# Gated mix of sliding-window attention and a gated feed-forward, forward and backward: Wo's gradient built in the last stage, and a new order of the first loads

## The chip, the cores and the metric

The kernel runs on one core of a Trainium2 chip. Times are device microseconds of one execution; the time of a kernel is the median over its runs. A profile is one further execution, recorded by the hardware; its span runs from the first to the last instruction of the program.

Engines: TensorE (PE in the profile; its weight loads are PEld), VectorE (DVE), ScalarE (ACT), GpSimd (POOL) and SyncE (SP), which here only issues transfers. Each engine works through its own instructions in order. A transfer is issued from the queue of one of them and is moved by 16 DMA engines.

## What is computed

With x of 2048 rows and 512 columns, 32 heads of 16, and a window of 256:

```python
g = sigmoid((x * gate_w).sum(-1))            # one gate a row
a = attention(x, wqkv, wo)                   # softmax(q k^T / 4 | window) v, then @ wo
b = ((relu(x@Wg)) * (x@Wu)) @ Wd             # F = 1376
out = g * a + (1 - g) * b
```

Returned are `out` and, for a given `grad_out` (go), the gradients of x, wqkv, wo, Wg, Wu, Wd and gate_w. With da = g * go and o the attention's output before `wo`, the gradient of wo is `o^T @ da`, a product of 512x2048 by 2048x512. It is this product that the change moves. Inputs and outputs are bf16.

## The kernel before

Rows are cut into NT = 16 tiles of 128; four tiles make a group (NTG = 4 groups of 512 rows). D = 512 is cut into DC = 4 chunks of 128 columns, which are also 4 chunks of 8 heads each; F into FC = 11 chunks, the last of which overlaps the one before.

**Start and stage 1** (to about 240 us of the profile): a program written out by hand, in which each engine's order is the order of the code. SP loads the first group of x in two halves (line 241); ScalarE's queue loads the first 256 columns of Wg and Wu (lines 242 and 243) and the gate's weights; SP goes on with x of group 1, a transpose of Wd's first chunk by DMA (`turn_wd`), and then by turns go and x of the groups (lines 255 to 262), and the rest of Wg and Wu. Per group `turn_x` transposes x on TensorE through a PSUM tile (two tiles of rows share one), VectorE copies the first half and ScalarE the second to `x_T`. `gate_col` gives the gate, `db_rows` multiplies go by 1 - g (lines 295 and 297, two of four tiles on each engine), `turn_db` transposes that. The main loop runs over 44 pairs of F's chunk and group; per pair it makes gate, up and dh products, multiplies them, transposes them by DMA, stores them to `hgu_d`, and adds up the weights' gradients. `make_da` makes da of a tile, and `turn_da` stores it to `da_d` in DRAM (line 320) and transposes it into `da_T` by DMA.

**Attention** (about 242 to 690 us): the four chunks of heads, one after another, each with 46 turns. A turn makes scores S and gradients of the probabilities D for four heads and two blocks, exp on ScalarE (line 747), masks on GpSimd (line 757), a product on VectorE (line 764), sums over rows on TensorE (lines 781, 783), transposes of the probabilities (TensorE at line 818, DMA at line 810), and pieces of dk and dv (lines 495, 498). The rows of dq, dk, dv and o of a chunk stand side by side in `rows_st` (`sts[c]`), which `spill` stores to `dqkvo_d`. One turn is written out behind the other; the position fixes the order on all queues.

Between these, background work is put in: `project_parts` of the next group, and the gradients of the chunk before, from `grad_parts`: four pieces for wqkv (384 columns, line 603) and, ahead of them, the part number DC for wo (512 columns, line 606). Each piece has a price in us; a credit per turn, from the prices left and the turns left, says how many pieces a turn gets. For wo's part, `grad_parts` loads all of da from `da_d` at turn 12 or so of each chunk: six loads of 256 KB on SP, two more from GpSimd's queue later (line 576). `late` holds weights for the last stage, one issued on every second turn.

**The seam** (about 690 to 711 us): no turns are left; the last chunk's gradients run (`early_group`, and `grad_parts` with `rest`). Its da comes by two loads of 512 KB (lines 871, 872) and four of 256 KB. The first group's data for the last stage are loaded by SP in the same stretch, W_up's last transposes behind them. `clear("Wu")` is a memset on GpSimd of the padded rows of what these transposes write.

**The last stage** (to the end): 16 tiles, in pairs that share loads (`load_group`, one pair ahead). Per tile TensorE makes bps = h Wd (11 matmuls, line 1117), aps = o wo (4, line 1121), and dx in `dxps` from 34 matmuls (lines 1147, 1173). From aps and bps come `out` and, by way of GpSimd's product with go (line 1133), the gate's derivative dz. VectorE adds dz's term to dxps (`dx_sb`, line 1179) and the rows of dx are stored. bps and aps have one PSUM buffer each, dxps has two. Here a scheduler may move instructions between engines' queues a little.

Of the kernel before, what the change touches and what calls it, by code (L numbers as in the profile page):

```python
# [22 lines left out]
def kernel(  # L23
# [20 lines left out]
    nc = tc.nc  # L44
# [54 lines left out]
    da_d = dram.tile([S, D], BF, name="da_d")  # L99
# [105 lines left out]
    with ExitStack() as p1, tc.manual_schedule():  # L205
# [36 lines left out]
        nc.scalar.dma_start(Wg_sb[:, :, 0:W0], Wg_v[:, :, 0:W0])  # L242
        nc.scalar.dma_start(Wu_sb[:, :, 0:W0], Wu_v[:, :, 0:W0])
# [27 lines left out]
        def turn_x(tg):  # L271
            for half in range(2):
                t0 = tg * TPG + 2 * half
                pt = ps1.tile([P, DC, 2, P], BF, tag="tr", bufs=2, name="ptx")
                for tt in range(2):
                    for c in range(DC):
                        nc.tensor.transpose(pt[:, c, tt, :], x_r[:, t0 + tt, c * P:(c + 1) * P], ident[:])
                evac(x_T[tg][:, :, 2 * half * P:(2 * half + 2) * P], pt[:].rearrange("p c t q -> p c (t q)"), ("dve", "act")[half])
# [40 lines left out]
        def turn_da(t):  # L319
            nc.sync.dma_start(da_d[t * P:(t + 1) * P, :], da_in[t][:])  # L320
# [150 lines left out]
    if True:  # L471
# [95 lines left out]
        def grad_parts(c, rest=None):  # L567
            out = []
            rows = {}

            def load_da(i, eng):
                pool, tag, bufs = (wk, "das", 2) if i in (4, 5) else (gwp, "dar", 4)
                a = pool.tile([P, 2, D], BF, tag=tag, bufs=bufs, name="dar")
                for e in range(2):
                    rows[2 * i + e] = a[:, e, :]
                eng.dma_start(a[:], da_d[i * 2 * P:(i + 1) * 2 * P, :].rearrange("(t p) d -> p t d", p=P))

            for i in range(6 if rest is None else 4):
                load_da(i, nc.sync)
            if rest is not None:  # L580
                rows.update(rest)
            hold = {}
            step = 2 if rest is None else 4

            def store(part, ws):
                if part < DC:
                    to = out_2[part * P:(part + 1) * P, :].rearrange("p (a n) -> p a n", a=3)[:, :, c * P:(c + 1) * P]
                else:
                    to = out_3[c * P:(c + 1) * P, :]
                return lambda: (nc.sync if rest is None else nc.gpsimd).dma_start(to, ws[:])  # L590

            def piece(part, t0, first, last):
                if first and rest is not None and part < DC:
                    if "SD"[part // 2] not in hold:
                        hold["SD"[part // 2]] = ps.tile([P, 2, 4, P], F32, tag="SD"[part // 2], bufs=1, name="wps")
                    hold[part] = hold["SD"[part // 2]][:, part % 2, 0:3, :]
                elif first:
                    hold[part] = ps.tile([P, 3, P] if part < DC else [P, D], F32, tag="tr", bufs=2, name="wps")[:]
                wps = hold[part]
                for t in range(t0, t0 + step):  # L600
                    go_, no_ = first and t == t0, last and t == t0 + step - 1
                    if part < DC:
                        nc.tensor.matmul(wps, lhsT=x_r[:, t, part * P:(part + 1) * P], rhs=sts[c][:, t, 0:3, :],  # L603
                                         start=go_, stop=no_)
                    else:
                        nc.tensor.matmul(wps, lhsT=sts[c][:, t, 3, :], rhs=rows[t], start=go_, stop=no_)  # L606
                if part == DC and rest is None and t0 + 12 < NT:
                    ev.setdefault(turn + 1, []).append(("load", lambda: load_da(t0 // 2 + 6, nc.gpsimd)))
                if not last:
                    return None  # L610
                if part < DC:
                    ws = (gwp if rest is None else S2["t6"]).tile([P, 3, P], BF, tag="ws", bufs=2 if rest is None else 5, name="ws")
                    share(ws[:], wps, 3 * P)
                    return store(part, ws)
                ws = (gwp if rest is None else S2["t6"]).tile([P, D], BF, tag="ws", bufs=2 if rest is None else 5, name="ws")
                share(ws[:], wps, D)
                return store(part, ws)

            if rest is None:
                parts = [(DC, 0, NT)] + [(p, 0, NT) for p in range(DC)]  # L620
            else:
                for a, b in ((0, NT - 4), (NT - 4, NT)):
                    if a:
                        out += [(DC, t0, t0 == 0, t0 + 4 == NT) for t0 in range(0, NT, 4)]
                    out += [(p, t0, t0 == 0, t0 + 4 == NT) for p in (0, 2, 1, 3) for t0 in range(a, b, 4)]
                return [lambda a=a: piece(*a) for a in out]
            for part, a, b in parts:
                out.append([(0.324 if part < DC else 0.432,
# [583 lines left out]
```

## Time and profile before

| | us |
|---|---|
| median of 3 runs | 894.38 |
| the runs | 887.89, 894.38, 899.25 |
| the profiled execution | 886.93 |
| its span | 885.2 |

Mean granted TensorE clock over the span: 0.998. Lines of the profile are read so: a group or a row names line, engine and operation, what it writes `<-` what it reads, and the shape; "x8" is how many instructions stand in a merged row; in a timeline the two numbers ahead are the start and the duration, and the bracket behind gives the idle time of the engine before it and what ended it. In the busy times by stretch, the numbers behind the stretch are its length and busy time (instructions) by engine, and at the end the granted clock, the mean share of time that the DMA engines were busy and GB/s. A row of transfers names destination and source, queue, count, size of one and the median time from issue to landing. Matmuls are pipelined: a 128x512 matmul has a duration of 379 ns in the records, while they start about 215 ns apart.

### The profile page before, as it was taken

Reading aid. Unit: us, or ns where it says so; the run is one execution under the profiler, and the core shown is the slowest. Engines: PE = TensorE matmul, PEld = TensorE weight load, DVE = VectorE, ACT = ScalarE, POOL = GpSimd, SP = SyncE. Lnnn points to the kernel's source line nnn. Section 1 sums busy time; section 2 is a strip of 40 time slices with the busy share of each in tenths; the row PEclk is TensorE's granted clock in tenths of the full one; section 3 lists DMA queues with packets and bytes.
Section 4 is the critical chain, followed back from the end, with each engine's and each line's share of the span. In section 5 each row is a group of like instructions: output and inputs, shape, how many; then the busy total and the mean of one; then the engine's idle time right before and its main releaser. Section 6 shows DMA issues by size and latency. Waiting matters only on the chain. (4 is left out here: it accounts for less than half of the span.)

```text
span 885.2 us, 29234 instructions
## 1 busy us (share of the span) xinstructions
PE 847.1 (96%) x12415; PEld 557.1 (63%) x12545; DVE 504.3 (57%) x758; ACT 386.2 (44%) x558; POOL 485.0 (55%) x894
## 2 busy tenths in 40 slices
PE   7999999999989999999999999999899999999998
PEld 4556655665557877777777767777677744444443
DVE  4445433333367888877778887787777323232222
ACT  5522222223266676766557655567455311111111
POOL 1645444444357787877668776687676532222221
PEclk9999999999999999999999999999999999999999
DMA  9999999998857999999978999899999999777750
GB/s 278 235 188 218 217 220 223 233 215 194 188 91 119 158 148 160 167 153 172 204 122 146 150 194 189 137 179 159 192 193 182 256 265 269 190 192 191 192 118 25
DMA packets 442156, 161.95 MB, mean 183 GB/s; under 512 B 361640, under 2 KB 439176, under 8 KB 442024
## 3 DMA queue, kind: packets, MB, share of 16 engines
q1 hardware_dynamic: 437896, 152.20, 90.9%
q0 software_dynamic: 2544, 7.34, 2.9%
q8 instruction: 98, 1.61, 0.7%
q10 hardware_dynamic: 1584, 0.53, 0.3%
q14 instruction: 34, 0.28, 0.1%
HBM read 38.44 MB, written 38.34 MB: 87 GB/s over the span
## 5 line engine op out<-in xcount | busy, mean ns | idle before, releaser
L764 DVE TENSOR_TENSOR PP<-PP,D 128x1024 bf16<-128x1024 bf16 (+1 forms) x184 | 219.2, 1191 | 68.2 <-POOL PP L757 24.7
L747 ACT ACTIVATE PP<-S 128x1024 bf16<-128x1024 f32 (+1 forms) x184 | 185.2, 1007 | 100.1 <-PE D L714 49.3
L757 POOL TENSOR_SCALAR_AFFINE_SELECT PP<-PP 128x512 bf16<-128x512 bf16 (+1 forms) x188 | 143.8, 766 | 90.1 <-ACT PP L747 87.4
L74 DVE COPY p<-pt 128x1024 bf16<-128x1024 bf16 x167 | 114.4, 685 | 13.0 <-PE pt L818 12.9
L357 POOL TENSOR_TENSOR hgu<-rg,upm 128x512 bf16<-128x512 bf16 x44 | 50.8, 1155 | 120.5 <-DVE upm L355 103.5
L818 PE MATMUL pt<-ident,PP 128*128 128x128 bf16 x1512 | 114.6, 219 | 0.9 <-issue 0.9
L781 PE MATMUL BA<-KV,PP 128*128 128x33 bf16 x1440 | 106.9, 180 | 3.7 <-ACT BAs L72 2.8
L781 PEld LDWEIGHTS <-PP 128*128 128x128 bf16 x1440 | 85.8, 96 | 31.1 <-issue 12.3
L783 PE MATMUL BA<-KV,PP 128*128 128x17 bf16 x1440 | 102.6, 170 | 0.7 <-issue 0.7
L397 PE MATMUL wps<-hgu_r,x_r 128*128 128x256 bf16 x640 | 96.0, 273 | 0.7
L495 PE MATMUL CD<-rq,p 128*128 128x32 bf16 x1440 | 94.9, 176 | 0.0
L498 PE MATMUL CD<-rq,p 128*128 128x16 bf16 x1440 | 93.6, 169 | 0.0
L783 PEld LDWEIGHTS <-PP 128*128 128x128 bf16 x1440 | 84.8, 96 | 10.7 <-issue 6.4
L818 PEld LDWEIGHTS <-PP 128*128 128x128 bf16 x1512 | 86.3, 97 | 1.2 <-issue 1.2
L714 PE MATMUL S<-zT,K 32*128 32x128 bf16 (+3 forms) x1056 | 77.9, 239 | 5.3 <-ACT PP L747 1.3
L495 PEld LDWEIGHTS <-p 128*128 128x128 bf16 x1440 | 80.7, 95 | 0.3
L498 PEld LDWEIGHTS <-p 128*128 128x128 bf16 x1440 | 80.5, 96 | 0.3
L397 PEld LDWEIGHTS <-x_r 128*128 128x128 bf16 x640 | 62.6, 98 | 28.6
L714 PE MATMUL D<-zT,V 32*128 32x128 bf16 (+3 forms) x1056 | 72.4, 238 | 5.8 <-DVE PP L764 5.2
L355 DVE SCALAR_TENSOR_TENSOR upm<-rg,ups 128x512 bf16<-128x512 bf16 x44 | 30.3, 689 | 79.8 <-PE ups L342 54.8
L1124 ACT COPY a_sb<-aps 128x512 f32<-128x512 f32 x16 | 9.4, 586 | 145.0 <-issue 133.1
L365 POOL TENSOR_TENSOR hgu<-dh_sb,rg 128x512 bf16<-128x512 bf16 x44 | 58.7, 1334 | 9.0 <-ACT dh_sb L363 9.0
(145 smaller groups left out, 1480.6 us busy)
## 6 DMA issues: line engine op xcount, KB each, us to landing
hgu_d<-hgu SPq DMA_DIRECT2D x44, 384.0 KB, 3.3
dqkvo_d<-rows_st SPq DMA_DIRECT2D x14, 512.0 KB, 4.7
dar<-da_d SPq DMA_DIRECT2D x22, 256.0 KB, 5.1
duT_g<-hgu_d SPq DMA_DIRECT2D x8, 640.0 KB, 6.0
dgT_g<-hgu_d SPq DMA_DIRECT2D x7, 640.0 KB
gt<-hgu_d SPq DMA_DIRECT2D x7, 640.0 KB, 5.9
p<-PP SPq DMA_TRANSPOSE x171, 4.2
out_dram<-wst SPq DMA_DIRECT2D x20, 128.0 KB, 3.0
```

The costliest lines, as they stand in the source:

```text
L74: nc.vector.tensor_copy(out, in_)
L365: nc.gpsimd.tensor_tensor(out=k.hgu[:, 2, :], in0=dh_sb[:], in1=k.rg[:], op=ALU.mult)
L397: nc.tensor.matmul(acc["w"][:, c, :], lhsT=x_r[:, t, c * P:(c + 1) * P], rhs=k.dgu_r[:, :, i, :], start=(go_ and c % 2 == 0), stop=no_, sk ...
L495: nc.tensor.matmul(cd[0][:, h, :], lhsT=p2[:, 0, pr, :], rhs=rq[:, h, 0:2 * Dh], start=cd[1], stop=True, skip_group_check=True)
L498: nc.tensor.matmul(cd[0][:, h, 0:Dh], lhsT=p2[:, 1, pr, :], rhs=rq[:, h, 2 * Dh:3 * Dh], start=False, stop=True, skip_group_check=True)
L714: nc.tensor.matmul(dst, lhsT=proj[(u.c, kb // TPG)][nm + ("", "1")[par]][rows[par], (kb % TPG) * P:(kb % TPG + 1) * P], rhs=proj[(u.c, qb ...
L747: nc.scalar.activation(two[:].rearrange("p x a b q -> p x a (b q)")[:, :, 0, 0:n], flat(us[0].S[:], n), ACT.Exp)
L757: nc.gpsimd.affine_select(out=out, in_=out, compare_op=ALU.is_ge, fill=0.0, base=0 if up else -1, pattern=[[0, 2], [0, b1 - b0], [1 if up ...
L764: nc.vector.tensor_tensor(out=v(1), in0=v(0), in1=flat(vs[0].D[:], n), op=ALU.mult)
L781: nc.tensor.matmul(BA[:, h, 0:33], lhsT=u.PP[:, 0, 2 * i + pr, :], rhs=kv[:, kb % TPG, h, 1:34], start=(first and pr == 0), stop=True, ski ...
L783: nc.tensor.matmul(BA[:, h, 33:50], lhsT=u.PP[:, 1, 2 * i + pr, :], rhs=kv[:, kb % TPG, h, 0:17], start=False, stop=True, skip_group_check ...
L818: nc.tensor.transpose(pt[:, a, b if u.nb == 2 else 2 * u.x + b, :], u.PP[:, a, b, :], ident[:])
```

## The change

Wo's gradient leaves `grad_parts` and is added up in the last stage, over all 16 tiles, in four PSUM tiles. da is made there anew by ScalarE from go (`da_b`), and o's rows come from `dqkvo_d` by a new load per tile (`o_g`). `da_d`, its 16 stores and all its loads go. To make room in PSUM, dxps has one buffer for two, and a small transpose at the end uses aps's. Of the new product, a tile's four matmuls are issued a tile later, behind aps of the next tile; the last tile's at once. At the last tile the four sums are copied (two on ScalarE, two on VectorE) and stored.

In the background work of attention, the part for wo is gone, the list of jobs per group of four tiles becomes (0, 2, 1, 1) for (0, 1, 2, 2), P2 has 14 buffers for 12, and in the last chunk `late` is issued on every fourth turn up to row tile 12.

At the start, all of x is issued ahead of Wd's transpose and of go; the first columns of Wg and Wu come behind the first group of x on SP and no more on ScalarE's queue; and the second half of the first group's copy to `x_T` is split between VectorE (two of four columns' chunks) and ScalarE.

```diff
-        nc.scalar.dma_start(Wg_sb[:, :, 0:W0], Wg_v[:, :, 0:W0])
-        nc.scalar.dma_start(Wu_sb[:, :, 0:W0], Wu_v[:, :, 0:W0])
+        nc.sync.dma_start(Wg_sb[:, :, 0:W0], Wg_v[:, :, 0:W0])
+        nc.sync.dma_start(Wu_sb[:, :, 0:W0], Wu_v[:, :, 0:W0])
...
-        load_x(1)
+        for tg in range(1, NTG):
+            load_x(tg)
         turn_wd(0)
-        load_go(0)
-        load_x(2)
-        load_go(1)
-        load_x(3)
-        load_go(2)
-        load_go(3)
+        for tg in range(NTG):
+            load_go(tg)
...
-                evac(x_T[tg][:, :, 2 * half * P:(2 * half + 2) * P], pt[:].rearrange("p c t q -> p c (t q)"), ("dve", "act")[half])
+                for c0, c1, eng in ((0, DC, "dve"),) if half == 0 else ((0, DC, "act"),) if tg else ((0, 2, "dve"), (2, DC, "act")):
+                    evac(x_T[tg][:, c0:c1, 2 * half * P:(2 * half + 2) * P],
+                         pt[:, c0:c1, :, :].rearrange("p c t q -> p c (t q)"), eng)
...
-            nc.sync.dma_start(da_d[t * P:(t + 1) * P, :], da_in[t][:])
...
-                p2 = pools["p2"].tile([P, 2, 4, P], BF, tag="P2", bufs=12, name="p2")[:]
+                p2 = pools["p2"].tile([P, 2, 4, P], BF, tag="P2", bufs=14, name="p2")[:]
...
+            o_g = S2["g6"].tile([P, GT, DC, P], BF, tag="o_g", name="o_g")
+            for t in range(GT):
+                t0 = (g * GT + t) * P
+                nc.sync.dma_start(o_g[:, t, :, :], dqkvo_d[t0:t0 + P, :].rearrange("p (c a n) -> p c a n", c=DC, a=4)[:, :, 3, :])
             nc.sync.dma_start(go_g[:] if g == 0 else go_g, go_d[gsl, :].rearrange("(t p) d -> p t d", p=P))
...
-                        for _ in range(((2, 1, 0, 0) if c == 0 else (0, 1, 2, 2))[j // TPG]):
+                        for _ in range(((2, 1, 0, 0) if c == 0 else (0, 2, 1, 1))[j // TPG]):
...
-                if late and (late[0] is not load_wo or turn > NI) and (not us or turn % 2 == 1):
+                if late and (late[0] is not load_wo or turn > NI) and (not us or turn % (4 if us[0].c == DC - 1 and us[0].q < 12 else 2) == 1):
...
+            wo_ps = [ps6.tile([P, D], F32, name=f"wo_ps{c}") for c in range(DC)]
+            pending_wo = []
+
+            def add_dwo(t_, o_, da_):
+                for c in range(DC):
+                    nc.tensor.matmul(wo_ps[c][:], lhsT=o_[:, c, :], rhs=da_[:], start=(t_ == 0), stop=(t_ == NT - 1))
...
+                    da_b = t6.tile([P, D], BF, tag="da_b")
+                    nc.scalar.mul(da_b[:], go_g[:, tl, :], g_all[:, t:t + 1])
+                    pending_wo.append((t, o_g[:, tl, :, :], da_b))
+                    while pending_wo and (pending_wo[0][0] < t or t == NT - 1):
+                        add_dwo(*pending_wo.pop(0))
                     a_sb = t6.tile([P, D], F32, tag="a_sb")
...
-                    dxps = ps6.tile([P, D], F32, tag="dxps", bufs=2)
+                    if t == NT - 1:
+                        for c in range(DC):
+                            ws = t6.tile([P, D], BF, tag="wo_s", bufs=DC, name="wo_s")
+                            evac(ws[:], wo_ps[c][:], ("act", "dve")[c % 2])
+                            nc.sync.dma_start(out_3[c * P:(c + 1) * P, :], ws[:])
+                    dxps = ps6.tile([P, D], F32, tag="dxps", bufs=1)
...
-                            dgw_t = ps6.tile([P, P], BF, name="dgw_t")
+                            dgw_t = psa.tile([P, P], BF, tag="aps", bufs=1, name="dgw_t")
```

In `grad_parts`, the loads of da (`load_da`, `rows`), the part number DC and its stores are taken out, and what is left keeps its order: four parts of 16 tiles for chunks 0 to 2, and in the seam the first twelve tiles of each part ahead of the last four.

More of the change, by code (lines that the diff above doesn't have):

```diff
@@ L599, in piece @@
                 wps = hold[part]
                 for t in range(t0, t0 + step):
[L601 to L606, printed above, removed]
@@ L607, in piece @@
-                if part == DC and rest is None and t0 + 12 < NT:
-                    ev.setdefault(turn + 1, []).append(("load", lambda: load_da(t0 // 2 + 6, nc.gpsimd)))
+                    nc.tensor.matmul(wps, lhsT=x_r[:, t, part * P:(part + 1) * P], rhs=sts[c][:, t, 0:3, :],
+                                     start=first and t == t0, stop=last and t == t0 + step - 1)
                 if not last:
                     return None
[L611 to L626, printed above, removed]
@@ L627, in grad_parts @@
[L627 to L631 removed]
+                ws = (S2["t6"] if seam else gwp).tile([P, 3, P], BF, tag="ws", bufs=4 if seam else 2, name="ws")
+                share(ws[:], wps, 3 * P)
+                to = out_2[part * P:(part + 1) * P, :].rearrange("p (a n) -> p a n", a=3)[:, :, c * P:(c + 1) * P]
@@ L936, in background @@
             def background():
[L937 removed]
+                price, f, more = bg.pop(0)
                 put = f()
```

75 lines of the change are left out of this document (24 added, 51 removed).

## The prediction

> **What bounds the kernel now.** I read the page's busy times first, then the busy times by stretch, then the chain of waits, and only then single engines.
>
> ```profile
> span 885.2 us, 29234 instructions
> ...
> PE 847.1 (96%) x12415; PEld 557.1 (63%) x12545; DVE 504.3 (57%) x758; ACT 386.2 (44%) x558; POOL 485.0 (55%) x894
> ```
> ```profile
> 0.00:20.00 20.00, 15.12 (x141) 9.29 (x144) 8.25 (x15) 10.45 (x16) 3.45 (x11) 1.00 0.99 266
> ...
> 100.00:140.00 40.00, 39.74 (x241) 23.90 (x245) 16.20 (x25) 11.62 (x20) 18.01 (x15) 1.00 0.96 223
> ...
> 348.10:462.50 114.40, 108.47 (x2496) 81.87 (x2518) 90.77 (x129) 70.86 (x98) 84.71 (x188) 1.00 1.03 163
> ...
> 735.00:885.00 150.00, 145.83 (x719) 67.17 (x732) 43.77 (x97) 16.88 (x30) 31.52 (x41) 1.00 0.67 164
> ```
>
> The columns after a stretch are its length and the busy time of TensorE, its weight loads, VectorE, ScalarE and GpSimd, then clock, DMA share, GB/s. TensorE fills stage 1 (39.74 of 40), attention for one chunk of heads at 95% (108.47 of 114.40) and the last stage at 97%. Only the first 20 us have much idle time, 4.9. So what the change is worth is, above all, how many matmuls it removes, and it removes none: 64 matmuls for Wo's gradient move from attention and the seam behind it into the last stage. Everything else is idle time gained or lost.
>
> **The change, part by part.** *Last stage.* Four matmuls 128x512 stand in each of 16 tiles.
>
> ```profile
> 703.47 1.32 PE wps L603 x8
> ...
> 705.06 3.18 PE wps L606 x14
> 708.24 1.30 PE wps L603 x8
> ...
> 723.79 0.86 PE aps L1121 x4
> 724.66 1.08 PE dxps L1147 x5
> ```
>
> In the chain four such matmuls take 0.86 us, and 64 take 64 x 0.215 = 13.8. TensorE is the bound there, so all of it is added: **+13.8**. At the seam (line 606, between the pieces of line 603) the 16 of the last chunk go: from 703.47 + 1.32 = 704.79 to 708.24, 3.45. They could have covered the wait for the last rows of k and v:
>
> ```profile
> 703.51 0.37 ACT L72 CAST rows_st<-CD 128x256 bf16<-128x256 f32 x1 [1.33 <-PE CD L498]
> ```
>
> That copy ends at 703.88, ahead of 704.79, so nothing is late next: **-3.45**.
>
> *Attention.* 48 matmuls leave it. Are they paid for there? These are TensorE's rows at the starts of two turns and of the turns after them, with the same pieces of dk and dv (24 pairs each), one turn with no background work and one with two dWo matmuls:
>
> ```profile
> 321.83 0.23 PE L714 MATMUL S<-zT,K 16*128 16x128 bf16 x2
> ...
> 323.74 0.23 PE L714 MATMUL S<-zT,K 16*128 16x128 bf16 x2
> ```
> ```profile
> 391.59 0.28 PE L714 MATMUL S<-zT,K 16*128 16x256 bf16 x2
> ...
> 393.60 0.38 PE L606 MATMUL wps<-dar,rows_st 128*128 128x512 bf16 x1
> 393.91 0.23 PE L714 MATMUL S<-zT,K 16*128 16x128 bf16 x2
> ```
>
> 1.91 us against 2.32: two matmuls cost 0.41, 0.205 each, the full rate. The one record at 393.60 stands for two; the other is missing. Thus 48 x 0.215 = 10.3 come off: **-10.3**. Bounds: nothing, if other turns are paced by VectorE, and 12, if the three copies of the sums also stood in the way.
>
> *The traffic.* These go:
>
> ```profile
> dar<-da_d SPq DMA_DIRECT2D x22, 256.0 KB, 5.1
> ...
> da_d<-da_t SPq DMA_DIRECT2D x16, 128.0 KB, 2.7
> ...
> dar<-da_d POOLq DMA_DIRECT2D x6, 256.0 KB, 6.2
> ...
> early<-da_d SPq DMA_DIRECT2D x2, 512.0 KB, 4.2
> ```
>
> That is 28 x 256 + 2 x 512 KB read and 2 MB written. Stage 1 has no idle time that the 16 stores could give back: 0. In the first two chunks with da loads no wait of TensorE ends on a transfer. In the last chunk one does, behind the loads that GpSimd issues beside the weights' transposes:
>
> ```profile
> 633.14 1.02 ACT L747 ACTIVATE PP<-S 128x1024 bf16<-128x1024 f32 x1 [2.18 <-DMA p<-PP]
> ```
> ```profile
> 635.08 0.52 PE L150 MATMUL pp<-x,p 128*128 128x512 bf16 x1 [1.17 <-ACT ws L72]
> ```
> ```profile
> 634.00:636.00 2.00, 0.92 (x7) 0.42 (x7) 0.51 (x2) 1.03 (x3) 1.69 (x5) 0.80 1.12 335
> 636.00:638.00 2.00, 2.00 (x60) 1.57 (x58) 1.08 (x1) 1.02 (x1) 0.33 (x2) 0.50 1.26 89
> 638.00:640.00 2.00, 1.60 (x11) 0.91 (x10) 0.83 (x2) 0.60 (x1) 1.29 (x3) 0.85 1.18 241
> ```
>
> ScalarE's exp waits 2.18 us until a transpose has read its tile; then the sum's copy of dWo is late and TensorE idles 1.17; then the clock is low: (0.20 + 0.50 + 0.15) x 2 = 1.7 us lost. With the loads, that copy and half of the weights' transposes (now on every fourth turn) gone from there, I count 1.17 + 1.7, rounded: **-3.0** (bounds 0 and -5). The wider P2 pool (14 buffers for 12) and the reordered jobs: 0; they alter when work is issued on queues, not how much TensorE has to do.
>
> Added in the last stage: 16 loads o_g of 128 KB in 256-byte pieces on SP. At the stage's 164 GB/s and share 0.67, 2.1 MB more over some 164 us are 13 GB/s; were these pieces four times as dear as the rest, the share would become 0.67 x (1 + 4 x 13/164) = 0.88, below one. Queued behind them on SP is only go_out's load of the same group, needed a group later, except for the first group. There ScalarE's da_b waits for go_g ahead of a_sb, but the next aps comes 10 us later: 0. The four copies of the finished sums at tile 15 lie beside that tile's 34 matmuls into dxps (7.3 us): 0.
>
> *One accumulator for dx where there were two.* dxps of a tile now waits for VectorE's dx_sb of the tile before. In general 19 matmuls (4.1 us) lie between, against one 0.75 us operation. Not so at tile 1:
>
> ```profile
> 719.93 0.52 POOL L529 MEMSET d<- 32x512 bf16 x1 [14.41 <-DMA d<-in_B_W_up_dram]
> 720.40 3.52 POOL L590 DMA_DIRECT2D out_dram<-ws  x5
> ...
> 723.92 1.73 POOL L1133 TENSOR_TENSOR amb<-amb,go_g 128x512 f32<-128x512 f32 x1
> ```
> ```profile
> 726.69 0.75 DVE L1179 SCALAR_TENSOR_TENSOR dx_sb<-gw_b,dz,dxps 128x512 bf16<-128x512 bf16 x1
> ```
> ```profile
> 686.91 2.21 SPq L576 DMA_DIRECT2D dar<-da_d  x4
> ```
>
> GpSimd waits for W_up's transposes, stores five sums, and only then multiplies for tile 0's gate; dx_sb of tile 0 ends at 727.44, and before, dxps of tile 1 had long begun (724.66). Now it would like to begin at 724.66 - 3.45 + 0.86 = 722.07. SP issues six loads fewer before those transposes (6 x 0.55) and two o_g more, so 2.2 earlier; one store fewer is 0.7: dx_sb ends at 724.5. **+2.4**, between 0 (the transposes land earlier still) and 4.7 (SP's time is not gained). The row at 636 shows that a stall of this size can bring the low clock, another 1.7, which I leave to the range. [...]
>
> *The start.* x's later groups now stand ahead of Wd's transpose and go_out.
>
> ```profile
> 3.71 0.57 SPq L229 DMA_DIRECT2D go_in<-in_grad_out_dram  x1
> 4.81 0.37 SPq L253 DMA_DIRECT2D x_r<-in_A_x_dram  x1
> ```
> ```profile
> go_in<-in_grad_out_dram SPq DMA_DIRECT2D x1, 512.0 KB, 8.1
> x_r<-in_A_x_dram SPq DMA_DIRECT2D x1, 512.0 KB, 8.6
> ```
> ```profile
> 12.41 1.27 DVE L297 TENSOR_SCALAR db_r<-go_in,omg_all 128x512 bf16<-128x512 bf16 x1
> ```
> ```profile
> 18.47 0.33 PE L277 MATMUL ptx<-ident,x_r 128*128 128x128 bf16 x3 [0.94 <-DVE db_T L74]
> ```
>
> The first go_out lands at 3.71 + 8.1 = 11.8, the next x at 4.81 + 8.6 = 13.4: 1.6 us for each 512 KB. Two groups of x ahead of it put go_out at 11.8 + 3.2 = 15.0, and db_r (line 297), which began at 12.41, cannot begin before. VectorE and ScalarE work in order: x_T of group 2 and everything up to db_T queue behind db_r, and TensorE's transposes at 18.47 wait for db_T. 2.6 us late there; I estimate that 0.6 comes back, because x and the second group's products are ready by then. **+2.0**, between -1.5 (go_out comes as soon as before, and the two waits for x go) and +3. The split copy of x gains half a microsecond at 7 us that this wait swallows.
>
> Sum: 13.8 - 3.45 - 10.3 - 3.0 + 2.4 + 2.0 = **+1.5**. The profiled execution took 886.93 (span 885.2 and 1.7 around it), so 888.4. That execution is faster than all three runs (887.89, 894.38, 899.25); what made those slower no trace shows. If stalls by transfers did, less traffic brings them nearer; so I add a fifth of the 7.45 us up to the median: **890**, against 894.38.
>
> **Rivals.** *The moved matmuls were free in attention* (slower). Place: the turns with dWo. If VectorE's chain paced them, 10.3 would not come off, while 13.8 is paid: 888.4 + 10.3 = 898.7, some 900 in a median run. It decides where a turn without its filler is no shorter than 2.3 us. For it: VectorE is 79% busy in the chunk; against it the two turns above.
>
> *Transfers cost more than one profile shows* (faster). The stalls at 633 recur in the slower runs in other chunks, each some 3 to 5 us with its low clock; without 10 MB of traffic they all go, and the start costs nothing: 886.93 + 13.8 - 3.45 - 10.3 - 8 = 879. For it: DMA share 1.03 in the chunk. Against: TensorE's share of 95% leaves little.
>
> *The start and tile 1 at their dear ends, each with a low clock*: 888.4 + 1.0 + 2.3 + 2 x 1.7 = 895.
>
> *The loads are not relieved*: x first means go_out last, the same bytes in another order; that is already in the sum as a loss.
>
> **How the numbers follow.** Forecast 0.60, free matmuls 0.15, more relief 0.13, dear ends 0.12. The range 880 to 901 takes in the rivals' times and the bounds of the unknown costs. 2% (18 us) is about what a measurement of this kernel can tell from no change. 876.5 needs relief beyond every stall I can find: 0.06. 912.3 needs the free-matmul case and stalls in most tiles of the last stage: 0.05. Within 2%: 0.89.
>
> **What would show it.** The last stage's tile is 0.86 longer and attention's second and third chunks are 3.4 shorter each and the last some 6; the seam has no line 606; no exp waits 2 us for a transpose near 630. At tile 1 TensorE waits for dx_sb; near 15 us db_r waits for a transfer. Wrong: a start without that wait, chunks as long as before (then the first rival), or waits of dxps in every tile.

## The result, and the profile after

The changed kernel has a median of 884.38 us over six runs (883.89 to 886.66), the kernel before 895.39 us over six (887.89 to 899.25). The ratio is 0.9892, 95% interval 0.9855 to 0.993: about 1.1% faster, inside the 2% that count as no change. Two things moved: the time, and its spread, 2.8 us in place of 11.4. The profiled execution of the changed kernel, one of its six, took 884.61; that of before took 886.93. So the two traces differ by 2.3 us only, a fifth of what the medians do. In the later batches the kernel before had medians of 893.69, 892.84 and 890.79, so what the change is worth depends on the batch, by up to 4.6 us.

The page's busy times, and the busy time by stretch for the stretches that the prediction showed of before:

```profile
span 882.9 us, 29350 instructions
...
PE 856.9 (97%) x12545; PEld 556.9 (63%) x12545; DVE 507.4 (57%) x764; ACT 394.5 (45%) x569; POOL 478.6 (54%) x887
```
```profile
0.00:20.00 20.00, 15.02 (x126) 9.02 (x127) 6.94 (x15) 8.77 (x14) 3.43 (x11) 0.91 0.94 284
100.00:140.00 40.00, 40.00 (x247) 23.93 (x245) 19.50 (x25) 11.02 (x19) 18.51 (x16) 1.00 0.92 201
349.30:458.70 109.40, 106.19 (x2500) 80.08 (x2496) 89.97 (x129) 70.27 (x96) 82.40 (x185) 1.00 0.97 151
720.00:882.00 162.00, 159.45 (x793) 72.95 (x791) 44.88 (x99) 26.49 (x46) 31.46 (x41) 1.00 0.65 163
```

The second chunk of heads (third row) is 5.0 us shorter than the 114.40 of before, with TensorE 97% busy. The last stage's tile, in the chain of waits, has the four new matmuls and no gap:

```profile
719.24 0.86 PE aps L1081 x4
720.11 0.86 PE wo_ps L1065 x4
720.97 4.75 PE dxps L1117 x22
```

Tile 1 of that stage, in the timeline of GpSimd, VectorE and TensorE (one fence, in this order):

```profile
702.32 0.51 POOL L526 MEMSET d<- 32x512 bf16 x1 [12.30 <-DMA d<-in_B_W_up_dram]
702.78 2.92 POOL L585 DMA_DIRECT2D out_dram<-ws  x4
705.20 1.05 POOL L1095 DMA_DIRECT2D out_dram<-o_sb  x1
705.77 1.66 POOL L1098 TENSOR_TENSOR amb<-amb,go_g 128x512 f32<-128x512 f32 x1
...
708.47 0.75 DVE L1149 SCALAR_TENSOR_TENSOR dx_sb<-gw_b,dz,dxps 128x512 bf16<-128x512 bf16 x1
...
709.27 1.02 PE L1117 MATMUL dxps<-x,f 128*128 128x512 bf16 x4 [1.91 <-DVE dx_sb L1149]
```

GpSimd issues its stores first and multiplies afterwards; TensorE waits 1.91 us for the dxps buffer. Earlier, at tile 0, TensorE already waits for the memset of W_up's padded rows, which it did not before:

```profile
702.88 0.38 PE L1117 MATMUL dxps<-d,duT_g 128*128 128x512 bf16 x1 [0.65 <-POOL d L526]
```

At the start, db_r waits for go_out's first load:

```profile
14.06 0.62 DVE L295 TENSOR_SCALAR db_r<-go_in,omg_all 128x512 bf16<-128x512 bf16 x2 [2.27 <-DMA go_in<-in_grad_out_dram]
```

The borders of the attention stage used here are the first scores of its first turn and of its last turn but one. These rows are from before, and then from after:

```profile
242.31 0.39 PE L714 MATMUL S<-zT,K 16*128 16x256 bf16 x4 [0.52 <-DVE KV L74]
...
685.61 0.23 PE L714 MATMUL S<-zT,K 16*128 16x128 bf16 x2
```
```profile
243.77 0.40 PE L674 MATMUL S<-zT,K 16*128 16x256 bf16 x4 [0.52 <-DVE KV L74]
...
670.30 0.23 PE L674 MATMUL S<-zT,K 16*128 16x128 bf16 x2
```

So the two executions differ by +1.46 up to the attention stage, 443.30 to 426.53 = -16.77 in it, and 199.59 to 212.60 = +13.01 from its last turn but one to the end: -2.3 in all.

The table gives the same borders for every kernel that was run, chunk by chunk (chunk 4 up to its last turn but one), and the time that exp on ScalarE waits in chunks 2 to 4 for a DMA transpose of the probabilities (PP), where the profile names one as what ended the wait. dWo is Wo's gradient.

| kernel (all in us) | da loads | start | chunk 1 | 2 | 3 | 4 | from last turn but one | exp waits for transposes |
|---|---|---|---|---|---|---|---|---|
| before | yes | 242.31 | 105.77 | 114.40 | 113.82 | 109.31 | 199.59 | 3.5 |
| before, again | yes | 241.98 | 105.74 | 116.72 | 115.89 | 108.08 | 201.99 | 1.7 |
| dWo's matmuls out | yes | 241.83 | 106.37 | 115.80 | 113.79 | 113.61 | 200.90 | 7.3 |
| loads spread out | yes | 242.60 | 105.76 | 114.85 | 113.91 | 113.85 | 203.33 | 6.5 |
| GpSimd's loads out | six of eight | 241.82 | 105.75 | 114.45 | 113.32 | 111.84 | 203.22 | 4.8 |
| no da loads | no | 242.03 | 105.76 | 113.69 | 113.30 | 106.20 | 199.42 | none |
| no loads, no matmuls | no | 242.43 | 105.74 | 112.75 | 111.87 | 104.79 | 199.12 | none |
| after | no | 243.77 | 105.54 | 109.41 | 109.23 | 102.35 | 212.60 | none |
| after, loads put back | such loads | 243.94 | 105.52 | 111.30 | 109.23 | 106.35 | 215.36 | 5.6 |
| after, 12 P2 buffers | no | 243.81 | 105.55 | 109.38 | 109.22 | 102.33 | 214.81 | none |
| after, old start | no | 241.87 | 105.54 | 109.40 | 109.01 | 102.30 | 213.78 | none |
| after, stores by ScalarE | no | 243.35 | 105.56 | 109.40 | 109.24 | 102.76 | 211.79 | 0.6 |
| after, old jobs | no | 243.42 | 105.54 | 109.09 | 109.13 | 102.43 | 211.89 | none |
| after, old start and stores | no | 243.66 | 105.53 | 109.39 | 109.00 | 102.17 | 210.95 | none |

### The profile page after: what moved, and what is told of

It reads as the page before. It is cut to its first block, busy times and chain, and to the rows that moved or that the text cites. A ratio compares the mean times of both kernels' runs of the same rounds, so it can differ in the third digit from the quotient of the medians.

```text
span 882.9 us, 29350 instructions
## 1 busy us (share of the span) xinstructions
PE 856.9 (97%) x12545; PEld 556.9 (63%) x12545; DVE 507.4 (57%) x764; ACT 394.5 (45%) x569; POOL 478.6 (54%) x887
## 5 line engine op out<-in xcount | busy, mean ns | idle before, releaser
L74 DVE COPY p<-pt 128x1024 bf16<-128x1024 bf16 x164 | 112.4, 685 | 10.7 <-PE pt L778 10.7
```

The costliest lines, as they stand in the source:

```text
L74: nc.vector.tensor_copy(out, in_)
```

## Experiments

The question after the result was why the medians differ by 11 us where two traces differ by 2.3. Theory A is the prediction's: the moved matmuls make the attention stage shorter. Theory B: the transfers of da cost far more in a typical run than in the profiled one. Theory C: the order of the background work and the P2 buffers. Each run below has times of the kernel before beside it, from the same chip.

**The kernel before, again.**

> The kernel before, unchanged. All theories: ratio 1.00 within its interval, and times again spread over 8 to 11 us. If its profiled execution falls on a slower one than the first (over 890), its turns show where the spread lies: by the theory of the transfers in the turns of the da loads (stalls of 1 to 2.5 us each, as at 633), by the theory of the clock in turns with a granted clock below 1, by the theory of the start ahead of 242 us.

892.49 (885.82 to 899.9, 10 runs) against 893.69, ratio 0.9976 (0.9941 to 1.001). The profiled execution, 892.14, is a slower one. Of the 5.2 us that it took more, 2.4 lie behind the last turn but one, and 3.1 in attention, ahead of which it gained 0.3. Attention is slower in turns 10 to 12 of its chunks (turns are counted from 0; SP issues the six da loads in turn 6, not in turn 12 or so as said ahead of the prediction). In the second chunk these rows stand there (timelines of ScalarE, TensorE and ScalarE):

```profile
373.33 1.02 ACT L747 ACTIVATE PP<-S 128x1024 bf16<-128x1024 f32 x1 [1.31 <-PE ptp L188]
...
374.41 0.28 PE L714 MATMUL S<-zT,K 16*128 16x256 bf16 x2 [1.16 <-ACT PP L747]
...
375.74 1.02 ACT L747 ACTIVATE PP<-S 128x1024 bf16<-128x1024 f32 x1 [0.90 <-DMA p<-PP]
```

The busy time by stretch around it:

```profile
372.00:374.00 2.00, 1.25 (x33) 1.16 (x29) 1.82 (x2) 0.69 (x2) 0.31 (x1) 1.00 1.29 258
374.00:376.00 2.00, 1.59 (x43) 1.48 (x43) 0.44 (x1) 1.10 (x3) 1.49 (x3) 0.77 1.09 112
376.00:378.00 2.00, 2.00 (x10) 0.90 (x9) 1.82 (x4) 1.15 (x2) 1.51 (x4) 0.50 1.10 183
378.00:380.00 2.00, 2.00 (x63) 1.68 (x62) 1.11 (x1) 1.62 (x2) 0.98 (x4) 0.87 1.10 213
```

A gap of TensorE, which waits for exp, and behind it a clock of 0.77, 0.50, 0.87. In the first profile the same turns ran without either. The profile puts the wait of the exp at 373.33 down to ptp, but in the first profile the same exp began at 372.46, ahead of its ptp (373.26). What it waited for is most likely the transpose that was issued behind the loads; the exp after it, at 375.74, names one. The transfers issued between 364.0 and 368.5, here and then in the run without da loads, show these transposes:

```profile
dar<-da_d SPq DMA_DIRECT2D x4, 256.0 KB, 6.0
p<-PP SPq DMA_TRANSPOSE x2, 8.2
```
```profile
p<-PP SPq DMA_TRANSPOSE x3, 3.4
```

The last figure is the median time from issue to landing: the transposes that SP issues behind the da loads land after 8.2 us, and without the loads after 3.4. In the first profile of before they took 6.9, and exp waited 0.25 us there: nearly the same stall, and no turn was longer for it.

**Before, without the da loads.** All of Wo's gradient is taken against x's rows; the 64 matmuls stay.

```diff
-            for i in range(6 if rest is None else 4):
-                load_da(i, nc.sync)
-            if rest is not None:
-                rows.update(rest)
+            rows.update({t: x_r[:, t, :] for t in range(NT)})
...
-                if part == DC and rest is None and t0 + 12 < NT:
-                    ev.setdefault(turn + 1, []).append(("load", lambda: load_da(t0 // 2 + 6, nc.gpsimd)))
...
-            out = [lambda: nc.sync.dma_start(rest[:, 0:4, :], da_v[:, 0:4, :]),
-                   lambda: nc.sync.dma_start(rest[:, 4:8, :], da_v[:, 4:8, :]), grads]
+            out = [lambda: None, lambda: None, grads]
```

> The kernel before, with Wo's gradient taken against x's rows, which lie in SBUF, instead of da: no da loads in the attention stage and the seam; its 64 matmuls stay where they are, and da is still stored. Theory A (the moved matmuls account for the shorter attention stage): 0 to 3 us faster than before, the spread of its times stays at 8 to 11 us. Theory B (the transfers and their waits cost more than one profile shows): 5 to 8 us off the attention stage, median near 885 to 888, and the spread shrinks to 3 us or less. Theory C (the order of the background work, the P2 buffers): no change.

882.65 (881.65 to 884.58), ratio 0.9869 (0.9834 to 0.9903), spread 2.9 us (6 runs) in place of 14.5 for before in the same batch (29 runs). The loads alone are worth 11 us in the median, as much as the whole change, and they make most of the spread. Theory B holds; the median came lower still than its 885 to 888. By traces alone the attention stage goes from 443.30 to 438.95, 4.35 us, and from the 446.43 of the second profile of before it is 7.5: the first profile had been a lucky execution.

**Before, with the loads but without 42 of the matmuls.**

```diff
-                    else:
+                    elif go_ or no_ or rest is not None:
                         nc.tensor.matmul(wps, lhsT=sts[c][:, t, 3, :], rhs=rows[t], start=go_, stop=no_)
```

> The kernel before, with the loads of da kept and 42 of the 48 matmuls of Wo's gradient in the attention stage left out (the first and the last of each of three products stay). Theory A: 42 x 0.215 = 9.0 us off the attention stage, about 3 in each of the last three chunks. Theory B: less, 3 to 6, since the waits for the loads stay, and the spread of 8 to 11 us stays. Rival that the matmuls were free in the attention stage: 0 to 1.

891.02 (886.22 to 895.4) against 893.69, ratio 0.9972 (0.9942 to 1.0002). Theory A's 9.0 us are excluded; chunk 3 is 113.79 beside 113.82 of before, not a moment shorter. The trace shows where the time went. Turns 18 to 20 of that chunk take 6.1 us in place of 7.3, and turn 21 takes 3.9 in place of 2.7. In turn 21 GpSimd issues its two da loads ahead of a mask, VectorE's product waits for the mask, and TensorE for the product (timelines of GpSimd, VectorE and TensorE, from chunk 3):

```profile
508.64 1.46 POOL L576 DMA_DIRECT2D dar<-da_d  x2
...
510.79 1.22 DVE L764 TENSOR_TENSOR PP<-PP,D 128x1024 bf16<-128x1024 bf16 x1 [1.27 <-POOL PP L757]
...
512.07 0.23 PE L714 MATMUL D<-zT,V 16*128 16x128 bf16 x2 [1.49 <-DVE PP L764]
```

In chunks 2 to 4 turn 21 takes 2.7 to 2.8 us in both profiles of before, and 2.2 in the two runs that keep the matmuls and have no loads of GpSimd's. So 0.5 to 0.7 us a chunk are the price of this issue in both, stall or not. Without the matmuls the price is higher: 3.9 to 4.0 here against 2.5 in the next run, which has no loads either. The profiled execution also has a stall of the loads in chunk 4, exp waiting 4.79 us for a transpose, so this run cannot price the matmuls by itself.

**The same without the loads.** It is the run without da loads with the matmul's line changed as above.

> The kernel before without da loads, and with 42 of the 48 matmuls of Wo's gradient in the attention stage left out, the rest in the order of before. To be set beside the run without da loads (882.65). Prediction's step (a matmul costs 0.215 us wherever it stands): 9.0 us faster, near 873.6. Rival that in this order they lay in time in which TensorE would wait for VectorE's PP at turn 21: 0 to 2 us faster, 880.5 to 882.7, with a wait of D for PP of some 1.7 us at turn 21 of each chunk; then the changed kernel's shorter chunks come from its order of the background work.

878.17 (876.95 to 880.47), ratio 0.9834 (0.9803 to 0.9864): 4.5 us under the run with matmuls in the medians (0.9 of it is also the difference of before between the two batches, 893.69 and 892.84), 3.8 in the attention stage of the traces. So a matmul left out *in its place* brought some 0.09 us, not 0.215: between theory and rival. Chunk 3 shows why. Turns 18 to 24 hold dWo's pieces, turns 25 to 45 those for wqkv. The rows give both stretches, first with the matmuls, then without them, then for the changed kernel:

```profile
501.70:518.90 17.20, 16.26 (x395) 12.03 (x398) 14.93 (x22) 9.77 (x12) 13.54 (x29) 1.00 1.11 159
518.90:574.80 55.90, 54.20 (x1196) 40.24 (x1197) 41.71 (x58) 32.66 (x46) 36.84 (x82) 1.00 0.97 165
```
```profile
501.20:516.90 15.70, 13.97 (x380) 11.34 (x384) 14.64 (x22) 9.73 (x12) 13.21 (x28) 1.00 1.11 161
516.90:572.80 55.90, 53.73 (x1189) 40.23 (x1195) 41.72 (x58) 32.66 (x46) 37.09 (x83) 1.00 1.04 165
```
```profile
498.70:517.70 19.00, 18.17 (x415) 13.77 (x418) 13.58 (x19) 10.43 (x15) 12.55 (x27) 1.00 0.87 152
517.70:568.00 50.30, 49.36 (x1164) 37.26 (x1166) 41.97 (x60) 31.96 (x43) 37.15 (x83) 1.00 1.09 169
```

Left out in place, the matmuls shorten their own turns by 1.5 us, TensorE's share there falls from 95% to 89% and VectorE's rises to 93%; the later turns stay at 55.9. In the changed kernel the list of background work is shorter, so wqkv's pieces move up into turns 18 to 24: that stretch becomes longer (19.0), and the later one 5.6 shorter. Together 73.1, 71.6 and 69.3. One more thing leaves with the change: in both runs TensorE waits once in turns 18 to 24 for the copy of the finished sum of dWo, 0.7 and 0.9 us, and the changed kernel has no such copy. So what a removed piece brings is set by the turns that its followers vacate, and by what goes with it. How the two divide is not shown: no run here changes one alone.

**After, with loads put back.** Eight of 256 KB a chunk, read from grad_out into tiles that nothing reads.

```diff
+            def load_da(i, eng):
+                pool, tag, bufs = (wk, "das", 2) if i in (4, 5) else (gwp, "dar", 4)
+                a = pool.tile([P, 2, D], BF, tag=tag, bufs=bufs, name="dar")
+                eng.dma_start(a[:], go_d[i * 2 * P:(i + 1) * 2 * P, :].rearrange("(t p) d -> p t d", p=P))
+
+            for i in range(0 if seam else 6):
+                load_da(i, nc.sync)
...
+                if part == 0 and not seam and t0 < 4:
+                    ev.setdefault(turn + 1, []).append(("load", lambda: load_da(t0 // 2 + 6, nc.gpsimd)))
...
-                p2 = pools["p2"].tile([P, 2, 4, P], BF, tag="P2", bufs=14, name="p2")[:]
+                p2 = pools["p2"].tile([P, 2, 4, P], BF, tag="P2", bufs=12, name="p2")[:]
```

> The changed kernel with transfers of the size and at about the places of the da loads put back into the attention stage (eight of 256 KB in each of three chunks, read from grad_out into tiles that nothing reads; 12 P2 buffers, to make room). Theory A: at most 3 us slower than the changed kernel (884.4), times still within 3 us of each other. Theory B: 889 to 892, with times spread over 8 us or more. Theory C (the P2 buffers matter): slower too, and told from B by a run with 12 P2 buffers alone.

889.81 (886.32 to 893.41, 12 runs), ratio 0.9947 (0.9918 to 0.9976): 5.4 us above the changed kernel, spread 7.1. Nothing reads these tiles, so it is the transfers themselves that cost, not a wait for da. In the trace, the time stands in turns 11 and 12 again, behind the burst of six: 1.9 us in chunk 2 and 3.3 in chunk 4. The next run makes the other edit, the P2 buffers, alone.

**After, with 12 P2 buffers.**

```diff
-                p2 = pools["p2"].tile([P, 2, 4, P], BF, tag="P2", bufs=14, name="p2")[:]
+                p2 = pools["p2"].tile([P, 2, 4, P], BF, tag="P2", bufs=12, name="p2")[:]
```

> The changed kernel with 12 P2 buffers, as before the change, in place of 14. By the prediction's step (nothing waits for a P2 buffer): no change, 884.4 within 1 us, so the 5.4 us that the transfers put back cost were those of the transfers. Rival (the buffers took away waits of the transposes): 3 to 6 us slower.

884.76 (883.32 to 886.76, 8 runs), ratio 0.9933 (0.9903 to 0.9962), with before at 890.79 in this batch. The chunks agree with the changed kernel's to 0.03 us. The buffers are worth nothing in the attention stage. The profiled execution, 886.76, is the slowest of the eight, and its extra 2.2 us lie in the last column (214.81). TensorE waits there for W_up's transposes and the memset of their padded rows, and behind these waits the clock is 0.59, where the changed kernel's trace has 1.00; at tile 1 it waits only 0.22 us for dx_sb (TensorE's timeline, then the stretch):

```profile
702.93 0.59 PE L1117 MATMUL dxps<-d,duT_g 128*128 128x512 bf16 x2 [1.15 <-DMA d<-in_B_W_up_dram]
705.06 0.38 PE L1117 MATMUL dxps<-d,duT_g 128*128 128x512 bf16 x1 [1.53 <-POOL d L526]
...
711.44 1.02 PE L1117 MATMUL dxps<-x,f 128*128 128x512 bf16 x4 [0.22 <-DVE dx_sb L1149]
```
```profile
705.00:709.00 4.00, 3.73 (x10) 1.46 (x11) 0.00 (x0) 0.00 (x0) 4.00 (x7) 0.59 1.25 231
```

**Before, with the six loads of SP spread over six turns.**

```diff
+            if rest is None:
+                for i in range(6):
+                    ev.setdefault(turn + 1 + i, []).append(("load", lambda i=i: load_da(i, nc.sync)))
+            else:
+                for i in range(4):
+                    load_da(i, nc.sync)
-            for i in range(6 if rest is None else 4):
-                load_da(i, nc.sync)
```

> The kernel before with all its da loads, but the six that SP issues in one burst at the seventh turn of a chunk are issued one in each of the next six turns. Theory Q (the transposes of PP queued behind the burst land late: 6.9 to 8.2 us after issue in place of 3.1 to 4.9, and exp waits for them): those transposes land within 5 us, no exp waits for one in turns 10 to 12, and the median falls by 3 to 7 us to 887 to 891; what is left of the 11 us are the two loads from GpSimd's queue, at turns 23 to 25 of the last chunk. Theory T (the 6.3 MB as such are too much for the stage, whenever they go): no change, 892 to 895 with the spread of 8 us or more.

891.18 (886.12 to 896.9, 12 runs) against 890.79, ratio 1.0017 (0.9988 to 1.0046). Theory Q was right about the place alone: no exp waits for a transpose in turns 10 to 12 of this trace, and the time is no better, as theory T has it. The stall stands at turn 23 of the last chunk, and it is the largest of all traces (ScalarE's timeline, then stretches):

```profile
635.50 1.02 ACT L751 ACTIVATE PP<-S 128x1024 bf16<-128x1024 f32 x1 [6.46 <-DMA p<-PP]
```
```profile
632.00:638.00 6.00, 1.43 (x39) 1.23 (x39) 0.54 (x2) 1.80 (x2) 1.41 (x2) 0.66 1.40 189
638.00:644.00 6.00, 5.33 (x76) 3.58 (x76) 3.21 (x5) 2.23 (x4) 3.19 (x9) 0.50 1.27 208
```

TensorE works 1.43 of 6 us, and then six at half its clock. In that chunk SP also issues the weights' transposes for the last stage.

**Before, without GpSimd's two loads.**

```diff
-                if part == DC and rest is None and t0 + 12 < NT:
-                    ev.setdefault(turn + 1, []).append(("load", lambda: load_da(t0 // 2 + 6, nc.gpsimd)))
...
-            if rest is not None:
-                rows.update(rest)
+            rows.update(rest if rest is not None else {t: x_r[:, t, :] for t in range(12, NT)})
```

> The kernel before with the two da loads that GpSimd issues in each of the last three chunks left out (rows 12 to 15 of Wo's gradient taken against x's rows instead); the burst of six on SP stays. Theory L (the two loads of the last chunk, among the transposes of zT and of W, hold back the transposes of PP, so that turns 23 to 25 take 8.6 us without and 10.6 to 15.6 us with them, by the run): turns 23 to 25 take 8.6, median 886 to 889, and the spread falls to 5 us or less. Theory Q (the burst of six matters more): 890 to 893, the spread stays at 8 us or more.

888.08 (885.02 to 892.1, 12 runs) against 892.84, ratio 0.995 (0.9925 to 0.9975), spread 7.1. The median came as theory L said, the spread (5 or less) and the place did not: turn 21 is 0.5 to 0.7 us shorter in each chunk, but turns 23 to 25 of the last chunk took 13.6 us in this execution (the slowest of the twelve), with no load of GpSimd's, while the second profile of before has 8.6 there with all the loads:

```profile
631.10 1.02 ACT L744 ACTIVATE PP<-S 128x1024 bf16<-128x1024 f32 x1 [4.06 <-DMA p<-PP]
```

SP's queue suggests why. These are its rows for the transpose of zT in the same turn, here and then in the run without loads:

```profile
621.12 2.46 SPq L176 DMA_TRANSPOSE rows<-zT  x1
```
```profile
617.05 1.30 SPq L176 DMA_TRANSPOSE rows<-zT  x1
```

SP is 4.1 us behind, the turns themselves only 1.0 (turn 20 of the chunk begins at 621.42 and at 620.43). It has not won back, among the weights' transposes, what it lost at the burst of six some 30 us earlier. No single load is to blame. Apart from turn 21, which of the loads costs how much in which run stays open.

**After, with the old start.** The three edits of the start are undone.

```diff
-        nc.sync.dma_start(Wg_sb[:, :, 0:W0], Wg_v[:, :, 0:W0])
-        nc.sync.dma_start(Wu_sb[:, :, 0:W0], Wu_v[:, :, 0:W0])
+        nc.scalar.dma_start(Wg_sb[:, :, 0:W0], Wg_v[:, :, 0:W0])
+        nc.scalar.dma_start(Wu_sb[:, :, 0:W0], Wu_v[:, :, 0:W0])
...
-        for tg in range(1, NTG):
-            load_x(tg)
+        load_x(1)
         turn_wd(0)
-        for tg in range(NTG):
-            load_go(tg)
+        load_go(0)
+        load_x(2)
+        load_go(1)
+        load_x(3)
+        load_go(2)
+        load_go(3)
...
-                for c0, c1, eng in ((0, DC, "dve"),) if half == 0 else ((0, DC, "act"),) if tg else ((0, 2, "dve"), (2, DC, "act")):
+                for c0, c1, eng in ((0, DC, "dve"),) if half == 0 else ((0, DC, "act"),):
```

> The changed kernel with the start of the kernel before: W's first columns on ScalarE's queue, grad_out's loads between those of x, the copy of x unsplit. By the step of the start as the traces have it (the attention stage begins at 243.77 in place of 242.31): 1.3 to 1.7 us faster than the changed kernel, near 882.9, with the times within 3 us of each other. Rival that the new start takes away the spread: times spread over 8 us again.

883.63 (882.32 to 885.71), ratio 0.9931 (0.9907 to 0.9954). In the trace db_r begins at 11.55 in place of 14.06, with no wait for go_in, and the attention stage at 241.87, 1.9 earlier; in the medians 0.75 is left beside the changed kernel, and 1.1 beside the run with 12 P2 buffers on the same chip. The spread stays small, so it is not the start that took it away.

**After, with the seam's stores on ScalarE's queue.**

```diff
-                return lambda: (nc.gpsimd if seam else nc.sync).dma_start(to, ws[:])
+                return lambda: (nc.scalar if seam else nc.sync).dma_start(to, ws[:])
```

> The changed kernel with the four stores of the seam on ScalarE's queue in place of GpSimd's. By the theory that GpSimd, which issues them only after its memset at 702.3, holds back amb and with it dz, dx_sb and the one dxps buffer at tile 1: amb starts 2 to 3 us earlier, the wait of 1.9 us for dx_sb goes, 1.5 to 2.6 us faster, near 882.3. Rival: the single dxps buffer alone sets the wait: no change.

883.76 (882.25 to 884.88), ratio 0.993 (0.9906 to 0.9953), 0.6 to 1.0 under the changed kernel and its run with 12 buffers, less than the 1.5 to 2.6 expected. The wait for dx_sb is gone, and amb follows the memset at once:

```profile
703.41 0.51 POOL L526 MEMSET d<- 32x512 bf16 x1 [13.37 <-DMA d<-in_B_W_up_dram]
703.88 0.55 POOL L1095 DMA_DIRECT2D out_dram<-o_sb  x1
704.44 1.17 POOL L1098 TENSOR_TENSOR amb<-amb,go_g 128x512 f32<-128x512 f32 x1
```

Here the memset itself came 1.1 us later, with W_up's transposes, which takes back a part of the 2.4 us gained between memset and amb (2.9 us in the changed kernel, 0.5 here).

**After, with the old order of jobs.**

```diff
-                        for _ in range(((2, 1, 0, 0) if c == 0 else (0, 2, 1, 1))[j // TPG]):
+                        for _ in range(((2, 1, 0, 0) if c == 0 else (0, 1, 2, 2))[j // TPG]):
...
-                if late and (late[0] is not load_wo or turn > NI) and (not us or turn % (4 if us[0].c == DC - 1 and us[0].q < 12 else 2) == 1):
+                if late and (late[0] is not load_wo or turn > NI) and (not us or turn % 2 == 1):
```

> The changed kernel with the order of before for the jobs of a chunk (0, 1, 2, 2 of them at its quarters, and a late transpose at every second turn) in place of 0, 2, 1, 1. The prediction put the order at nothing: within 1 us of the changed kernel (884 to 885.5). Rival (the new order is what makes the changed kernel's chunks 4 us shorter than those of the run without da loads): 6 to 12 us slower, 890 to 896.

883.83 (883.2 to 887.32), ratio 0.9901 (0.987 to 0.9932). No change: theory C falls, and with it the rival that the new order made the chunks short.

**After, with both cures.**

The old start, and the seam's stores on ScalarE's queue.

> The changed kernel with the start of before and the seam's stores on ScalarE's queue, both together. If the two gains add up (each some 1 us in its own run): 882.0 to 883.0, 1.5 to 2.5 us under the changed kernel. Rival (the start's gain is lost in waits at the seam): 883.5 to 884.5.

882.27 (881.11 to 882.67), ratio to before 0.9876 (0.9844 to 0.9908), 1.6 under the run with the old jobs on the same chip and 2.1 under the changed kernel. It is the fastest of the versions that leave nothing out. The trace cannot divide the gain, for in this one execution the old start came no earlier (attention from 243.66). It was not go_out: db_r began at 13.81, right behind the gate's values (omg_all), without a wait for it. TensorE had waited 1.10 us for a copy of x and 0.95 for x's next load, and its clock was 0.80, 0.50 and 0.85 from 8 to 14 us, where the run with the old start alone has 1.00.

## Why the prediction came out as it did

The time lies in the range, within 2% of before, and 5.6 us under the forecast of 890. In order of its steps:

*Last stage, seam and tile 1* (+13.8 - 3.45 + 2.4 = +12.75): measured +13.01. The tile is 0.86 longer and the seam has no piece of wo. Tile 1 waited for dx_sb as forecast, 1.91 us for 2.4, and the cause was the one named, GpSimd's stores ahead of its product. The "nothing is late next" of the seam was not so: with the seam's 3.45 us gone, TensorE waits 0.65 us for W_up's padded rows, a term that the sum lacks. With both as measured it is 13.8 - 3.45 + 1.91 + 0.65 = 12.9. That the stall at tile 1 would draw a low clock was left to the range: the busy time shows a clock of 1.00 behind it (below); the 0.59 in the trace with 12 P2 buffers follows the waits for W_up's rows, 1.15 and 1.53 us, instead. In the second trace of before, a gap of 1.16 us stands ahead of 0.77 and 0.50. So in these traces the length of a gap alone does not tell which stall is followed by the low clock.

*Attention* (-10.3): this is the step that was mis-sized, in two ways. From the run without da loads to the changed kernel the stage goes from 438.95 to 426.53, -12.4, just outside the bounds of 0 and 12. The prediction saw two matmuls cost 0.41 us in one pair of turns and took the full rate for all 48. Left out in place, a matmul brings about 0.09, so the first rival, free matmuls, was half right about its mechanism; and yet the moved ones brought 0.26 each, because the list behind them closed up and the copies of the three sums went with them. The copies were in the upper bound, the move to other turns was in no term of the sum. The two errors have opposite signs, and 2.1 us are what they left; that the sum came so near here is luck. The chunks came 5.0, 4.6 and 7.0 us shorter between the two traces, where the prediction named 3.4, 3.4 and some 6.

*Traffic* (-3.0, bounds 0 to -5): -4.35 between traces, inside the bounds. Some 1.8 of it are turn 21 in three chunks, GpSimd's issue of its loads, which no term of the sum has; the stall at 633 was the term. And the sum started from one execution of before that had met few of these stalls. Over the runs the loads cost 0.0131 x 893.69 = 11.7 us (8.7 to 14.8 by the interval). The prediction saw that the profiled execution was faster than every run, asked what the others had met, and allowed "a fifth of the 7.45 us" towards the median. In fact all of that gap went with the loads: the changed kernel's profiled execution (884.61) stands at its median (884.38). The second rival had the mechanism, stalls as at 633 that recur in other chunks with their low clock, and 3 to 5 us for each. Its 879 was too low for two reasons: it took 8 us off the one execution that had hardly paid them, where the traces give 4.35 (the matmuls made up 2.1 of that), and it left out the start and the waits at tiles 0 and 1.

*Start* (+2.0): +1.46. db_r waits for go_in as expected, until 14.06 where some 15 was forecast, 1.65 us later than before and not 2.6. Behind this stall the clock fell, to 0.56 and 0.59 from 16 to 20 us; two runs with the same start (stores by ScalarE, old jobs) kept 1.00 there and reach attention at 243.35 and 243.42, some 0.4 us earlier than the 243.77 here. The prediction had a low clock behind this stall in its rival of the dear ends only. Undoing the start gave 1.9 in the trace and about 1 in the median.

*Put at nothing*: P2's buffers and the order of jobs, rightly by two runs. The split copy was not tried alone.

By the sum: attention and traffic -16.77 for -13.3, start +1.46 for +2.0, the rest +13.01 for +12.75, together 3.8 lower, 888.4 to 884.6; the other 1.8 are the allowance towards the median, with the rounding.

## What to carry to other kernels

If the profiled execution is faster than the runs, find the places where its queues nearly failed (a transpose that landed just in time) before you price a change by it; a change can be worth most in executions that you have not seen. Transfers can cost through the others that they make late, even when nothing waits for them (here 5.4 us in the median, with loads into tiles that nothing reads), and moving some of them out of the way may only move the stall: here spreading six of them brought nothing, taking all of them out 11 us. And price a removed piece of background work by the turns that get emptied at the end of the list and by the copies that go with it, not only by the turn in which it stood.

## What the hardware showed unexpectedly

Transposes on SP's queue landed 3.4 us after issue on their own and 8.2 (6.9 in the first profile) behind six loads of 256 KB, in the same turns. The exp that waits for them did so in all six traces with such loads, 1.7 to 7.3 us in total by the waits that the profile names so, and in the eight without them for 0.6 in one and not at all in seven.

The granted clock followed such gaps without a rule that these traces show: 0.50 behind a gap of 1.2 us in attention, and 1.00 through the longer one, 1.9 us, at tile 1 of the changed kernel, by its busy time there:

```profile
707.00:709.00 2.00, 0.36 (x2) 0.08 (x1) 1.50 (x5) 0.71 (x2) 0.43 (x1) 1.00 1.30 286
709.00:711.00 2.00, 1.73 (x9) 0.78 (x9) 1.47 (x3) 0.00 (x0) 1.39 (x3) 1.00 1.03 240
```

Even the same stall can do either. Behind the start's wait for go_out, these are the same stretch of the changed kernel and of its run with the old jobs:

```profile
16.00:18.00 2.00, 1.18 (x12) 1.18 (x12) 1.68 (x3) 0.97 (x3) 1.15 (x1) 0.56 1.10 350
```
```profile
16.00:18.00 2.00, 1.27 (x17) 1.09 (x18) 1.67 (x3) 0.97 (x3) 1.15 (x1) 1.00 1.11 350
```
